# One fused kernel of attention with memory and a gated feed-forward: the hand-written order of GpSimd, VectorE and TensorE around the nested products is changed

## The chip, the cores and the metric

The kernel runs on one core of a Trainium2 chip. The metric is the device time of one execution, in microseconds (us); the number given for the kernel before is the median of three runs. One further execution was recorded by the hardware profiler, and all rows below come from it. The engines are named as the profile names them: PE is TensorE (PEld its weight loads), DVE is VectorE, ACT is ScalarE, POOL is GpSimd and SP is the engine that issues the transfers.

## The reference

The input x has 2048 rows of D = 576. Two branches are computed from it and mixed row by row by a gate:

```python
def _A_ref(x, wq, wk, wv, wo, beta):          # 32 heads of 18, 4 segments of 512 rows
    ...
    for s in range(N):
        qs, ks, vs = q[:, :, s], k[:, :, s], v[:, :, s]
        logits = jnp.einsum("bhqd,bhkd->bhqk", qs, ks) * scale + mask
        p = _softmax(logits, axis=-1)
        a_dot = jnp.einsum("bhqk,bhkd->bhqd", p, vs)
        pq = phi(qs)
        num = jnp.einsum("bhld,bhde->bhle", pq, M)
        den = jnp.einsum("bhld,bhd->bhl", pq, z)[..., None] + 1e-6
        a_mem = num / den
        o = g * a_mem + (1.0 - g) * a_dot
        outs.append(o)
        pk = phi(ks)
        M = M + jnp.einsum("bhld,bhle->bhde", pk, vs)
        z = z + jnp.einsum("bhld->bhd", pk)
    ...
    return o @ wo

def _B_ref(x, w_gate, w_up, w_down):          # F = 4608
    return (_gelu(x @ w_gate) * (x @ w_up)) @ w_down

g = _sigmoid((x * gate_w).sum(-1, keepdims=True))
return g * _A_ref(...) + (1 - g) * _B_ref(...)
```

The softmax is over the 512 keys of one segment; what lies before the segment enters through the memory M and its norm z.

## The kernel before, in words

All large products are made in 16-bit floats, and each 32-bit operand is split into two of them: a high half (a rounded copy, written by ACT) and a low half (the rest, written by POOL as operand minus high half). A pair of halves is what a product reads. "High" and "low" in a function's name (`high_g`, `low_g`, `high_d`, `low_d`, `hidden_pair`, `nest_pairs`) mean these two.

The program has three parts. At its start (to about 250 us) come the projections of the four segments, the memory and the pairs of x. The main part is a row of 72 steps, `step(v)`. Two steps make one block of 128 of the 4608 hidden columns (`f = v // 2`), over two row segments each (`p = v % 2`); four steps make a period (`fb = v // 4`, `i4 = v % 4`). Beside it each step from the fifth on works on one head of the attention, two tiles of it (`2k`, `2k + 1`, with `k = v - 4`). The last part holds what is left of the down product and the output projection.

In a step, PE makes the gate and up products of a block as seven products of a two-by-two split (A11, A12, A22, S1, S2, S4 and further sums of weights times x or sums of x; `product`, line 529) in the PSUM banks V, G (called X in the code) and U (called Y). DVE copies and adds them into the buffers `gl` (three of them) and `hold`, ACT takes the gelu in place, and `hidden` (DVE, line 1260) multiplies the up product in. `hidden_pair` (lines 1265 and 1266) then makes the two halves `hh` at the start of the next step, in `end_pair`.

For the blocks of even f the first product of a block is itself split once more (the nested variant): `nest(at, 0)` to `nest(at, 3)` are four pieces of it, made a step ahead in the steps i4 = 3 and i4 = 0, and `nest_last` is the fifth, made in the step that uses it. The pieces need sums of the raw weights (POOL, lines 327 to 387), and four nest pairs of these (`nest_pairs(b, i, "hl")`, high half on ACT in line 375, low half on POOL in line 377). The pieces gather in `hold0` (opened in step i4 = 3, read in the next period, and read last as a hidden tile in its fourth step) and `hold1`. There is one buffer of each. The first piece writes it with the copy in line 1361 of DVE.

The attention of a tile goes PE (scores, `st`/`dn` banks) -> DVE (maximum, line 1155) -> ACT (line 1166, `mb`; line 1171, the exponentials `pb`; line 1172, their high half `ph`) -> POOL (line 1173, low half) -> SP (transposing transfers) -> PE (values, line 1190). `powers(a)` is the part on ACT and POOL, `scores` and `put` that of PE and DVE, `values` the last.

The down product is cut into chains (`some(fb - 1, ...)`, 8 to a step, those of a period behind; line 1237), each of six matmuls and one eviction on DVE (line 1245). The down weights come by `load_d` (SP), are scaled by `scale_d` (DVE, line 391) and split by `high_d` and `low_d` (ACT line 395, POOL line 399); the buffers are two for the raw ones and four for the pairs. `squares` (ACT, line 89) gathers the column norms of coming weights and `scales` (PE, line 94, one matmul with ones) turns them into scale factors. `result_high` and `result_low` (ACT line 1214, DVE line 1220) split the attention's finished columns.

The order of work on PE, ACT, DVE and POOL is the order in which the code issues it: the program is built with a schedule written by hand for these four engines. Only SP's order is left to the scheduler. So a call that is moved in the code is moved on each of the four engines, and an engine never works past an instruction that waits.

## Time and profile before

| | us |
|---|---|
| median of three runs (lowest, highest) | 1604.89 (1604.72, 1605.11) |
| the profiled execution | 1603.99 |
| its span, first to last instruction | 1602.3 |
| PE busy | 1568.8 (98%) |
| PE weight loads busy | 953.8 (60%) |
| DVE busy | 1271.0 (79%) |
| ACT busy | 1208.5 (75%) |
| POOL busy | 1117.8 (70%) |

The granted TensorE clock is 0.999 on average. A row of a timeline gives start and duration in us, engine, line, operation, output and input, size and, in brackets, the idle time before it with what ended it; several like instructions in a row stand as one with a count. In the list of waits, the numbers are the total in us, how often, and the longest.

### The profile page before, as it was taken

The page shows a single profiled execution, that of the slowest core. Times are in us where ns is not written, and L with a number is a line of the kernel's source. Part 1 is how long each engine was busy: PE and PEld are TensorE (multiplying, and loading weights), DVE is VectorE, ACT ScalarE, POOL GpSimd, SP SyncE. Part 2 cuts the span into 40 slices and gives each one's busy share as a digit, 9 for nine tenths or more (in the row PEclk, how much of TensorE's full clock was granted, in tenths as well). Part 3 has the DMA queues.
Part 4 walks back from the last instruction along what each step waited for, and adds up shares of the span by engine and source line. Part 5 has one row for each costly group of instructions (what it writes and reads, how often), then busy time and mean ns, then how long its engine had stood idle before and what let it go on. Part 6 is the DMA issues. An engine that isn't in the chain of part 4 may idle for free. (4 is left out here: it accounts for less than half of the span.)

```text
span 1602.3 us, 33969 instructions
## 1 busy us (share of the span) xinstructions
PE 1568.8 (98%) x12220; PEld 953.8 (60%) x12220; DVE 1271.0 (79%) x3254; ACT 1208.5 (75%) x2059; POOL 1117.8 (70%) x1220
## 2 busy tenths in 40 slices
PE   9999998999999999999999999999999999999999
PEld 5665654565555555555565555555555556555577
DVE  6778975878788888888787878888888878787665
ACT  7567543879797889888887979788988888786421
POOL 5255555678686868686867868686868686776597
PEclk9999999999999999999999999999999999999999
DMA  6533332577776777777767778777777776764546
GB/s 228 208 123 130 124 122 56 112 117 133 130 135 127 131 142 131 126 138 125 134 128 131 129 129 138 130 136 134 138 130 140 127 138 131 131 115 92 119 85 168
DMA packets 472833, 209.97 MB, mean 131 GB/s; under 512 B 427688, under 2 KB 437416, under 8 KB 472152
## 3 DMA queue, kind: packets, MB, share of 16 engines
q1 hardware_dynamic: 472664, 207.80, 64.3%
q8 instruction: 96, 1.57, 0.4%
q14 instruction: 73, 0.60, 0.1%
HBM read 91.87 MB, written 27.26 MB: 74 GB/s over the span
## 5 line engine op out<-in xcount | busy, mean ns | idle before, releaser
L1173 POOL TENSOR_TENSOR pb<-pb,ph 128x896 f16<-128x896 f32 (+1 forms) x256 | 368.6, 1440 | 295.7 <-ACT ph L1172 285.6
L529 PEld LDWEIGHTS <-pairg 128*128 128x128 f16 x2592 | 249.3, 98 | 266.1 <-issue 27.6
L1237 PE MATMUL dn<-paird,hhr 128*128 128x288 f16 x2124 | 326.7, 286 | 0.3 <-DVE mx L1155 0.3
L1171 ACT ACTIVATE pb<-pb,mb,esc 128x512 f32<-128x512 f32 (+3 forms) x512 | 305.0, 642 | 5.3
L1245 DVE SCALAR_TENSOR_TENSOR acc<-dn,ev,acc 128x288 f32<-128x288 f32 x534 | 265.9, 513 | 42.3 <-PE dn L1237 34.4
L1237 PEld LDWEIGHTS <-hhr 128*128 128x128 f16 x2160 | 207.3, 98 | 87.8 <-issue 12.8
L529 PE MATMUL G<-x,pairg 128*128 128x512 f16 x864 | 211.1, 380 | 6.3 <-DVE gl L1260 6.3
L529 PE MATMUL U<-xt,pairg 128*128 128x512 f16 x864 | 209.9, 379 | 0.0
L1237 PE MATMUL dn<-paird,hhd 128*128 128x288 f16 x1272 | 204.8, 286 | 0.0
L1172 ACT ACTIVATE ph<-pb 128x896 f16<-128x896 f32 (+1 forms) x256 | 188.5, 736 | 8.1
L342 POOL TENSOR_TENSOR pairg<-raw,pairg 128x384 f16<-128x384 f32 (+2 forms) x144 | 158.5, 1122 | 13.9 <-ACT pairg L338 13.9
L1155 DVE CUSTOM_DVE_ANT_0 pb<-st,mask 128x512 f32<-128x512 f32 (+1 forms) x256 | 157.0, 613 | 0.0
L1237 PEld LDWEIGHTS <-hhd 128*128 128x128 f16 x1296 | 124.9, 98 | 49.8 <-issue 5.7
L1166 ACT ACTIVATE mb<-mx,esc 128x4 f32<-128x4 f32 x128 | 37.3, 291 | 149.2 <-DVE mx L1155 149.2
L1155 DVE CUSTOM_DVE_ANT_0 pb<-dn,mask 128x256 f32<-128x256 f32 (+1 forms) x192 | 67.1, 374 | 78.2 <-PE dn L1152 78.2
L1345 PE MATMUL V<-xt,nest 128*128 128x256 f16 x714 | 109.1, 273 | 13.1 <-POOL nest L377 12.2
L1269 ACT ACTIVATE gl<-gl,sc 128x512 f32<-128x512 f32 x110 | 75.2, 712 | 49.2 <-DVE gl L1513 37.6
L529 PE MATMUL V<-x,pairg 128*128 128x512 f16 x426 | 103.8, 379 | 2.4 <-DVE gl L1430 0.9
L529 PE MATMUL U<-x,pairg 128*128 128x512 f16 x432 | 105.0, 379 | 0.1
L1345 PEld LDWEIGHTS <-nest 128*128 128x128 f16 x714 | 64.4, 97 | 50.0 <-POOL nest L377 16.9
L1190 PEld LDWEIGHTS <-pt 128*128 128x128 f16 x2560 | 83.4, 96 | 5.5
L1266 POOL TENSOR_TENSOR hhr<-gl,hhr 128x512 f16<-128x512 f32 x67 | 78.6, 1183 | 11.5 <-ACT hhr L1265 11.5
(364 smaller groups left out, 3126.5 us busy)
## 6 DMA issues: line engine op xcount, KB each, us to landing
raw<-in_wgu_dram SPq DMA_DIRECT2D x36, 640.0 KB
rawd<-in_wd_dram SPq DMA_DIRECT2D x36, 288.0 KB
qt<-qk SPq DMA_DIRECT2D x132, 72.0 KB
kt<-qk SPq DMA_DIRECT2D x132, 72.0 KB
qk<-stage SPq DMA_DIRECT2D x36, 256.0 KB
qt<-qk SPq DMA_DIRECT2D x132, 36.0 KB
kt<-qk SPq DMA_DIRECT2D x132, 36.0 KB
vp<-vstage SPq DMA_DIRECT2D x16, 296.0 KB
```

The costliest lines, as they stand in the source:

```text
L342: pool.tensor_tensor(spot(f, *p, 1), raw_g[f][:, p[0] : p[1]], spot(f, *p, 0), OP.subtract)
L529: pe.matmul(o, w[:, i, (a + k) * P : (a + k + 1) * P], x[:, b + k], start=start and k == 0 and i == 0 and b == h, stop=k == 1 and i == 1, ...
L1155: dve.tensor_tensor_reduce(scored(a, qi), out[qi], mask[:, L - (qi + 1) * P :], 1.0, -3e38, OP.add, OP.max, mx[a][:, qi : qi + 1])
L1171: act.activation(r, r, AF.Exp, bias=b[:, qi : qi + 1], scale=esc[:, 0, c : c + 1])
L1172: act.activation(h[:, cols], p, AF.Copy)
L1173: pool.tensor_tensor(low[:, cols], p, h[:, cols], OP.subtract)
L1190: pe.matmul(ov, pr[:, 10 * i + COL[qi] // P + kb], v[:, 4 * e + kb, c0 : c0 + VC], start=kb == 0 and i == 0, stop=kb == qi and i == 1)
L1237: pe.matmul(o[:, :NH], hh[:, a, q * P : (q + 1) * P], w[:, b, n * NH : (n + 1) * NH], start=i == 0, stop=i == 5)
L1245: dve.scalar_tensor_tensor(av, o[:, :NH], ev, av, OP.mult, OP.add)
L1266: pool.tensor_tensor(hh[:, 1], t, hh[:, 0], OP.subtract)
L1269: act.activation(t, o, AF.Gelu_apprx_tanh, scale=scl[f // 2][0][:, 2 + c : 3 + c])
L1345: pe.matmul(o, w[:, (7 * c + i) * P : (7 * c + i + 1) * P], x[d], start=start and n == 0, stop=n == 2, skip_group_check=True)
```

## The change

It has six parts.

1. In the main part, the fourth step's start used to make the low halves of its two hidden tiles on POOL at once. Now `hidden_pair` may leave them (`wait=True`), and `hidden_lows` makes them after the step's `powers(2 * k - 1)`. The pair of down weights that was split in the third step is split in the fourth, with the other one. In the third step, the first two nest pairs and the sums that follow are made before `powers(2 * k)` instead of after; the third pair comes at the end of the third step, the fourth in the fourth step behind the hidden lows.
2. The down weights are loaded in the first step of their own period, both, instead of in the third and fourth step of the period before.
3. `result_low` is issued one step sooner, in the third step instead of the fourth.
4. In the steps i4 = 0 and 1, two chains follow the last nested piece, instead of one there and one further on.
5. `scales` of the next period is called after the next product and chain instead of before.
6. In the first period the nest pairs are made at the end of step 2 and the hidden low of step 2 behind them; the nest pieces of step 3 come one place later each; the first down weights are split at step 3's start; among the first projections, two value weights are split by other engines and one query/key pair is split in two calls.

The diff, with comments and the parts that only rename left out:

```diff
@@ make_v, the first projections
-            if k < 3:
+            if k not in (2, 3):
                 pair_of(t, r, sc)
                 return
...
-                    if 2 <= j < 6:
+                    if j == 4:
+                        make_qk(7, pair_high)
+                        finish_later()
+                        make_qk(7, pair_low)
+                    elif 2 <= j < 6:
                         make_qk(j + 3)
...
-                    if 1 <= j < 6:
+                    if 1 <= j < 5:
                         make_v(j - 1)
+                    if j == 4:
+                        make_v(4)
@@ hidden_pair
-        def hidden_pair(f, c, t):
+        def hidden_pair(f, c, t, wait=False):
             slot = hh_slot[f, c] = hh_free.pop(0)
             hh = hp[f, c] = hh_tile(slot)
             act.activation(hh[:, 0], t, AF.Copy)
-            pool.tensor_tensor(hh[:, 1], t, hh[:, 0], OP.subtract)
+            lows.append((hh, t))
+            if not wait:
+                hidden_lows()
+
+        def hidden_lows():
+            while lows:
+                hh, t = lows.pop(0)
+                pool.tensor_tensor(hh[:, 1], t, hh[:, 0], OP.subtract)
@@ weights_nest
-            if i4 == 2 and at == 2:
+            if i4 == 2 and at == "late":
                 for i in range(2):
                     nest_pairs(fb + 1, i, "hl")
                 nest_sums(fb + 1)
+            if i4 == 2 and at == 2:
+                for i in (2,) if fb else (2, 3):
+                    nest_pairs(fb + 1, i, "hl")
             if i4 == 3 and at == 0:
-                for i in (2, 3):
-                    nest_pairs(fb + 1, i, "hl")
+                hidden_lows()
+                if fb:
+                    nest_pairs(fb + 1, 3, "hl")
@@ weights_low, weights_load
-            if i4 >= 2:
-                low_d(n0 + i4 - 2)
+            if i4 == 3:
+                for f in (n0, n0 + 1):
+                    low_d(f)
...
-            if i4 == 2:
-                load_d(n0 + 2)
+            if i4 == 0 and fb:
+                load_d(n0)
+                load_d(n0 + 1)
             if i4 == 3:
                 load_g(n0 + 5)
-                load_d(n0 + 3)
@@ step
-            low = (k - 7) // 4 if k % 4 == 3 and 0 <= (k - 7) // 4 < H // 2 - 1 else None
+            low = (k - 6) // 4 if k % 4 == 2 and 0 <= (k - 6) // 4 < H // 2 - 1 else None
...
-            end_pair()
+            end_pair(i4 == 3 and fb > 0)
             if v == 3:
                 high_g(2, 1)
                 low_g(2, 1)
+                for n in range(2):
+                    high_d(n)
+                    low_d(n)
...
-            if v != 4:
-                some(fb - 1, early[:1])
+            one = 2 if fb and i4 < 2 else 1
+            some(fb - 1, early[:one])
...
-            if v in (2, 3):
-                nest_pairs_x(v - 2, 1)
+            if v == 2:
+                nest_pairs_x(0, 1)
             weights_nest(fb, i4, 1)
-            if v == 3:
-                nest(at, 0)
-            some(fb - 1, early[0 if v == 4 else 1 : 2])
+            some(fb - 1, early[one:2])
...
-            if v == 0 or fb > 1 and i4 == 1:
+            if v == 0:
                 scales(fb + 1)
                 scales_out(fb + 1)
...
             if v == 3:
-                nest(at, 1)
+                nest(at, 0)
             some(fb - 1, early[2:3])
-            if v == 5:
-                scales(2)
-                scales_out(2)
+            if fb and i4 == 1:
+                scales(fb + 1)
+                scales_out(fb + 1)
             product(Y, f, S1, t, 0, 2)
             rest(Y, f, G4, x2_, (0,) if fb else (0, 1))
+            if v == 3:
+                nest(at, 1)
...
-            if v == 3:
-                nest(at, 2)
             if not fb:
                 hidden(f, c, X, g0)
-                hidden_pair(f, c, g0)
+                hidden_pair(f, c, g0, v == 2)
...
             product(Y, f, S4, x2_, 2, 6)
+            if v == 3:
+                nest(at, 2)
...
             put(2 * k, 2)
             puts.pop(2 * k, None)
+            weights_nest(fb, i4, "late")
             if on(k):
                 powers(2 * k)
...
             ends.append((f, e, Y, g1))
+            if v == 3:
+                nest_pairs_x(1, 1)
             weights_nest(fb, i4, 2)
+            if v == 2:
+                hidden_lows()
```

How this moves instructions is seen at three places of a period from the middle of the main part. The first is POOL at the end of the third step and in the fourth (`pb` are the attention's low halves, `hhr` the hidden ones, `nest` the nest pairs' low halves; numbers tell buffers' uses apart). Before:

```order
L387 TENSOR_TENSOR raw<-raw 128x128
L1266 TENSOR_TENSOR hhr_11682<-gl,hhr_11682 128x512
L1266 TENSOR_TENSOR hhr_11685<-hold_10728,hhr_11685 128x512
L1173 TENSOR_TENSOR pb_11648<-pb_11648,ph 128x896
L1173 TENSOR_TENSOR pb_11648<-pb_11649,ph 128x384
L377 TENSOR_TENSOR nest<-nest 128x256
L377 TENSOR_TENSOR nest<-raw,nest 128x256
L342 TENSOR_TENSOR pairg<-raw,pairg 128x384
```

And now:

```order
L387 TENSOR_TENSOR raw<-raw 128x128
L1179 TENSOR_TENSOR pb_11542<-pb_11542,ph 128x896
L1179 TENSOR_TENSOR pb_11542<-pb_11543,ph 128x384
L377 TENSOR_TENSOR nest<-nest 128x256
L1179 TENSOR_TENSOR pb_11656<-pb_11656,ph 128x896
L1179 TENSOR_TENSOR pb_11656<-pb_11657,ph 128x384
L1281 TENSOR_TENSOR hhr_11684<-gl,hhr_11684 128x512
L1281 TENSOR_TENSOR hhr_11686<-hold_10727,hhr_11686 128x512
L377 TENSOR_TENSOR nest<-raw,nest 128x256
```

The hidden tiles' low halves went from ahead of the tile's attention product to behind it, the other tile's attention product from before the nest's first pairs (not shown) to behind them, and the two later nest pairs apart from each other.

The second is ACT in the third step, up to the attention's `mb` (waits in brackets). Before:

```order
L395 ACTIVATE paird<-rawd 128x576
L1269 ACT_TABLE_LOAD
L1269 ACTIVATE hold_10728<-hold_10728,sc 128x512 [waits DVE_49]
L1269 ACTIVATE gl<-gl,sc 128x512 [waits DVE_49]
L1166 ACTIVATE mb<-mx,esc 128x4 [waits DVE_49]
L1171 ACT_TABLE_LOAD [waits DMAHW3_49,Activation_49]
```

And now:

```order
L395 ACTIVATE paird<-rawd 128x576
L1284 ACT_TABLE_LOAD
L1284 ACTIVATE hold_10727<-hold_10727,sc 128x512 [waits DVE_49]
L1284 ACTIVATE gl<-gl,sc 128x512 [waits DVE_49]
L375 ACTIVATE nest<-raw 128x256 [waits Pool_49]
L375 ACTIVATE nest<-nest 128x128 [waits Pool_49]
L1172 ACTIVATE mb<-mx,esc 128x4 [waits DVE_49]
```

The high halves of the first two nest pairs, which wait for POOL, now stand ahead of `mb`.

The third is DVE in the fourth step, from the attention's maximum to the first hidden product of the pair. Before:

```order
L1361 COPY hold_11852<-V 128x256 [waits PE_49,Pool_49]
L1245 SCALAR_TENSOR_TENSOR acc<-dn,ev,acc 128x288 [waits PE_49]
L1155 ISA pb_11811,mx<-st,mask 128x384
L1155 ISA mx 128x1
L1364 COPY hold_11852<-V 128x256 [waits PE_49]
L1365 COPY V<-V 128x256 [waits DVE_49]
L1245 SCALAR_TENSOR_TENSOR acc<-dn,ev,acc 128x288 [waits PE_49] x2
L1369 TENSOR_TENSOR hold_11852<-V,hold_11852 128x256 [waits PE_49]
L1220 SCALAR_TENSOR_TENSOR ob<-ob,wsc,oh 128x576
L1260 SCALAR_TENSOR_TENSOR gl<-G,sc,gl 128x512 [waits PE_49,Activation_49]
```

And now:

```order
L1381 COPY hold_11851<-V 128x256 [waits PE_49,Activation_49,Pool_49]
L1251 SCALAR_TENSOR_TENSOR acc<-dn,ev,acc 128x288 [waits PE_49]
L1161 ISA pb_11810,mx<-st,mask 128x384
L1161 ISA mx 128x1
L1384 COPY hold_11851<-V 128x256 [waits PE_49]
L1385 COPY V<-V 128x256 [waits DVE_49]
L1251 SCALAR_TENSOR_TENSOR acc<-dn,ev,acc 128x288 [waits PE_49] x2
L1389 TENSOR_TENSOR hold_11851<-V,hold_11851 128x256 [waits PE_49]
L1266 SCALAR_TENSOR_TENSOR gl<-G,sc,gl 128x512 [waits PE_49,Activation_49]
```

The result's low half (L1220) left its place ahead of the hidden product. The copy into the hold buffer waits for POOL before and now; the last POOL reader of that buffer is the second of the two hidden low halves above (`hold_10728` before, `hold_10727` now, the same single buffer).

More of the change, by code (lines that the diff above doesn't have):

```diff
@@ L1260, in hidden @@
             dve.scalar_tensor_tensor(t, o, sc[:, 6 + c : 7 + c], t, OP.mult, OP.mult)
-        def hidden_pair(f, c, t):
+        lows = []
+        def hidden_pair(f, c, t, wait=False):
             slot = hh_slot[f, c] = hh_free.pop(0)
@@ L1381, in end_first, with end_pair @@
             ends[0] = ends[0] + (True,)
-        def end_pair():
+        def end_pair(wait=False):
             for i, g in enumerate(ends):
@@ L1392, in end_pair @@
             for f, c, o, g, *_ in ends:
-                hidden_pair(f, c, g)
+                hidden_pair(f, c, g, wait)
             ends.clear()
@@ L1514, in step @@
             gelu(f, e, g1, g1)
-            if v == 3:
-                for n in range(2):
-                    high_d(n)
-                    low_d(n)
             if fb:
@@ L1526, in step @@
                 normalize(k - 2)
-            if v == 3:
-                nest(at, 2)
             if not fb:
                 hidden(f, c, X, g0)
-                hidden_pair(f, c, g0)
+                hidden_pair(f, c, g0, v == 2)
                 if v < 3:
```

## The prediction

> **What bounds the kernel now.** I read the page's busy shares first, then the waits of PE, then one period of four steps in the timeline. One matrix engine does nearly everything:
>
> ```profile
> span 1602.3 us, 33969 instructions
> PE 1568.8 (98%) x12220; PEld 953.8 (60%) x12220; DVE 1271.0 (79%) x3254; ACT 1208.5 (75%) x2059; POOL 1117.8 (70%) x1220
> ```
>
> PE is idle for 33.5 us of the span, so that is about all that a change of order can win. The waits of PE say where:
>
> ```profile
> PE V L1345 <- POOL nest L377: 12.2, 17, 4.9
> PE G L529 <- DVE gl L1260: 6.3, 17, 0.4
> PE dn L94 <- ACT nest L89: 3.2, 15, 0.2
> ...
> PE dn L419 <- POOL wv L606: 0.8, 1, 0.8
> ```
>
> Sixteen of the first wait, fifteen of the second and third come once in each period of four steps; the longest, 4.9 us, is step 3. One period, from its third step's end to the next period's start, on PE:
>
> ```profile
> 854.90 0.71 PE L1345 MATMUL V<-xt,nest 128*128 128x256 f16 x5
> 856.09 0.28 PE L1345 MATMUL V<-xt,nest 128*128 128x256 f16 x1 [0.48 <-POOL nest L377]
> 856.96 0.49 PE L1345 MATMUL V<-xt,nest 128*128 128x256 f16 x3
> 860.94 0.66 PE L1190 MATMUL pv<-vt,pt 128*128 128x37 f16 x20
> 861.97 1.46 PE L529 MATMUL G<-x,pairg 128*128 128x512 f16 x6 [0.38 <-DVE gl L1260]
> 863.59 0.90 PE L1237 MATMUL dn<-paird,hhr 128*128 128x288 f16 x6
> 864.54 1.46 PE L529 MATMUL V<-x,pairg 128*128 128x512 f16 x6
> ```
>
> The idle time in brackets leaves out the drain of the matmuls before it, so I count starts. Three nest matmuls start over 0.33 us, twenty pv over 0.50, six dn over 0.73. The nest's sixth matmul then comes 0.64 late, G 0.53 late, and V after the chain 0.22 late.
>
> **The change, part by part.** Three losses are removed by moving work.
>
> First, G waits for DVE, which stands on the result's low half before the hidden product:
>
> ```profile
> 860.45 0.81 DVE L1220 SCALAR_TENSOR_TENSOR ob<-ob,wsc,oh 128x576 f16<-128x576 f32 x1
> 861.18 0.74 DVE L1260 SCALAR_TENSOR_TENSOR gl<-G,sc,gl 128x512 f32<-128x512 f32 x1
> 863.79 0.69 DVE L1430 COPY gl<-V 128x512 f32<-128x512 f32 x1 [0.33 <-PE V L1345]
> ...
> 841.27 0.75 DVE L1260 SCALAR_TENSOR_TENSOR gl<-G,sc,gl 128x512 f32<-128x512 f32 x1 [0.37 <-PE G L1279]
> 842.68 1.46 PE L529 MATMUL G<-x,pairg 128*128 128x512 f16 x6
> ```
>
> The 0.81 goes to the step before, ahead of that step's hidden product, which DVE starts at 841.27 after 0.37 idle. So it starts 0.44 later and ends at 842.46, and PE writes G again at 842.68: covered by 0.2 us, I cost it at nothing, and at 0.4 per period if that cover is gone. Gain 15 x 0.54 = 8.1 us.
>
> Second, V waits for the copy L1430, which ends 0.69 after 863.79, at 864.48. With two chains (1.47 us) instead of one, PE arrives at 865.06. The second chain is taken from ahead of the next product, where six matmuls (1.46 us with the last one's end) still cover DVE's 0.69 copy. Gain 0.21 x 32 steps = 6.7 us.
>
> Third, the scales' sum (L94) waits for ACT's squares:
>
> ```profile
> 812.21 0.90 PE L1237 MATMUL dn<-paird,hhd 128*128 128x288 f16 x6
> 813.32 0.39 PE L94 MATMUL dn<-stat,ones 128*128 128x10 f32 x2 [0.21 <-ACT nest L89]
> ```
>
> It is 813.32 - 812.94 = 0.38 late and moves behind eight matmuls and a chain, about 2.25 us. Gain 15 x 0.38 = 5.7 us.
>
> The fourth edit is GpSimd's order, and it is the one in question. It removes the nest's stall of 0.64 x 16 = 10.2 us, since the third pair's low half is there long before. But it also puts the low half of the hidden tile that lies in the hold buffer behind both attention products. That buffer is single, and the copy at line 1361 (1381 now), which opens the next hold, waits for GpSimd. So I follow GpSimd and ACT through it:
>
> ```profile
> 838.84 1.28 POOL L399 TENSOR_TENSOR paird<-rawd,paird 128x576 f16<-128x576 f32 x1
> 840.08 0.74 POOL L327 TENSOR_TENSOR raw<-raw 128x256 f32<-128x256 f32 x1
> 844.29 2.89 POOL L1173 TENSOR_TENSOR pb<-pb,ph 128x896 f16<-128x896 f32 x2
> 850.29 1.16 POOL L1266 TENSOR_TENSOR hhr<-gl,hhr 128x512 f16<-128x512 f32 x1
> 851.40 1.16 POOL L1266 TENSOR_TENSOR hhr<-hold,hhr 128x512 f16<-128x512 f32 x1
> 855.36 0.67 POOL L377 TENSOR_TENSOR nest<-nest 128x256 f16<-128x256 f32 x1
> ...
> 839.91 0.30 ACT L1166 ACTIVATE mb<-mx,esc 128x4 f32<-128x4 f32 x1 [0.53 <-DVE mx L1155]
> 843.01 0.95 ACT L1172 ACTIVATE ph<-pb 128x896 f16<-128x896 f32 x1
> 845.30 0.40 ACT L375 ACTIVATE nest<-raw 128x256 f16<-128x256 f32 x1
> 845.60 0.29 ACT L375 ACTIVATE nest<-nest 128x128 f16<-128x128 f32 x1
> 845.80 0.61 ACT L1265 ACTIVATE hhr<-gl 128x512 f16<-128x512 f32 x1
> 846.84 0.28 ACT L1166 ACTIVATE mb<-mx,esc 128x4 f32<-128x4 f32 x1
> 848.60 0.95 ACT L1172 ACTIVATE ph<-pb 128x896 f16<-128x896 f32 x1
> ...
> 856.48 0.42 DVE L1361 COPY hold<-V 128x256 f32<-128x256 f32 x1 [1.05 <-PE V L1345]
> ```
>
> - GpSimd's sums move up by the removed L399, 1.24 us: they took 840.08 to 844.29, and now end at 843.05.
> - ACT's first two nest halves now stand ahead of the attention's mb, and the second waits for those sums. So mb starts near 843.34, not 839.91: **3.43 us later**.
> - From mb to the end of the first ph is 4.05 us: 847.39. GpSimd's attention product takes 847.46 to 850.30 (2.84 of its 2.89 us pass before the next one starts). The third pair's low half follows and is done at 850.94, not 856.03.
> - ACT's attention block takes 5.39 us (839.91 to 845.30), then one nest half (0.31) and two hidden halves (1.04): the second mb is at 850.08, its ph ends 2.71 later, at 852.79.
> - GpSimd's second product: 852.87 to 855.71. Only now come the two hidden low halves, 2.23 us: **857.94**. Before they ended at 852.5.
> - The copy, for which PE is ready at 855.84 (856.48 less 0.64) when the nest's stall is gone, starts at 858.00 and PE's next nest matmuls 0.48 after it, as the rows of before have it: 858.5. Before it was 856.96, so this place gets 1.57 us longer although the old stall is gone. PE's new wait is 858.5 - 856.3 = **2.2 us**.
>
> Queued behind the copy on DVE stand a chain's eviction, half of an attention maximum and two more copies, 2.3 us in all; PE waits for the first copy alone, since twelve dn matmuls and twenty pv (1.47 + 0.50 us) stand between its second and its third nest piece, and the piece itself takes 0.33. Price: 16 x 1.57 = +25.1 us. From below: if ACT's and GpSimd's blocks pack tighter by 1.57 us, nothing; from above, if DVE's work stretches GpSimd's two products by a tenth each, 0.6 us: 9.3 us more.
>
> **Step 3**, where the first hold is opened, is separate. The last two rows are stretches of time: length, then busy us (and instructions) of PE, its weight loads, DVE, ACT and GpSimd, the granted clock, the DMA share and GB/s:
>
> ```profile
> 251.80 0.39 PE L1345 MATMUL V<-xt,nest 128*128 128x256 f16 x2 [0.60 <-ACT nest L375]
> 257.12 0.40 PE L1345 MATMUL V<-xt,nest 128*128 128x256 f16 x1 [4.93 <-POOL nest L377]
> 257.31 2.77 PE L529 MATMUL G<-x,pairg 128*128 128x512 f16 x6
> 268.06 1.46 PE L529 MATMUL V<-x,pairg 128*128 128x512 f16 x6 [0.85 <-DVE gl L1430]
> 253.17:256.58 3.41, 0.00 (x0) 0.00 (x0) 1.39 (x1) 0.25 (x1) 3.41 (x4) 1.00 0.00 0
> 256.58:260.00 3.42, 2.88 (x8) 1.17 (x9) 0.42 (x1) 0.00 (x0) 1.15 (x2) 0.50 0.30 64
> ```
>
> The waits cost 0.60 + 4.93 + 0.85, and 1.31 (2.77 less 1.46) for six matmuls at the granted clock 0.50: 7.7 us. Now the pairs are made in step 2, but a deferred hidden low half (1.16 us in the rows above) stands behind them on GpSimd, and the step's first U copy on DVE waits for it. From above all 7.7 us are won; from below nothing, if the waits only move. I take two waits in their place, each of one low half and one DVE copy (1.16 + 0.69 = 1.85 us): at the product that writes U again, and at the next one, which the nest's own copies stand ahead of. They are the nearest rows, and both too short for the clock to fall as it did. Gain 7.7 - 3.7 = 4.0 us.
>
> The down weights' loads go from the third and fourth step to the first one of their own period. ACT's squares read them in the second step, about a quarter period after the issue; I cost them at nothing, and if they land late it is the squares, and ACT's attention block behind them, that wait. The reorder among the first projections concerns the 0.8 us that PE waits for value weights from GpSimd. PE's next work there hangs on DVE's staging, which is not shortened: I cost it at nothing, at best 0.8.
>
> Sum: +25.1 - 8.1 - 6.7 - 5.7 - 4.0 = **+0.6 us**. The profiled execution took 1603.99 (span 1602.3); the median of the runs is 1604.89, 0.9 above. Forecast: no change, **1605.5 us**.
>
> The stretch at clock 0.50 began after a window of 3.41 us without one matmul. The Trainium skill (TensorE: Matmul & The Clock Gate, What's actually happening) says that the clock halves after at least one whole idle window of some 3.4 us; the trace agrees at step 3. By that rule a wait of 2.2 us cannot halve it, and the sum stands; it speaks against the second rival below.
>
> **The rivals.** *The new wait is short or hidden*: ACT and GpSimd finish the attention products some 2 us sooner than in my chain. For it: mb in before sat 0.53 us idle and the chain assumes that nothing else gives. Against it: every link is a start-to-start distance of the trace. Then the period loses 0.64 + 0.54 + 0.42 + 0.38 = 1.98 us, 16 x 1.98 + 4.0 = 36: **1569 us**; with half the wait, **1587**.
>
> *The clock falls (slower)*: if PE's 2.2 us wait, once in each period, draws a half-clock window as 4.93 us did, each costs up to 1.31 us more: 16 x 1.31 = +21, **1626 us**. It decides only when the wait covers a window; against it, the waits are 1.2 us short of one.
>
> *The small waits come back*: V, G and L94 wait for the same amount at the next place, since DVE and ACT have the same work. Then 20.5 us of gain shrinks to half: **1615 us**. Against it: DVE shows idle time of 1.05 and 0.33 us right there.
>
> **How the numbers follow.** What a measurement can tell from no change is about 0.2%, 3.2 us. The new wait has an error of 0.3 us in sixteen periods, 4.8 us. The forecast's case has 0.65: of it 0.33 within 0.2%, 0.18 faster, 0.14 slower. The short wait has 0.17, all faster; the clock 0.08, slower; the returning waits 0.10, slower but for 0.02. In all: faster 0.35, same 0.35, slower 0.30. The likeliest case alone spans 1597 to 1613; the range, with the half wait and the returning waits, 1586 to 1616.
>
> **What would show it.** Right: PE waits of about 2.2 us sixteen times at the nest, put down to the hold copy, the copy waiting for GpSimd's hidden low half; mb of the first head some 3.4 us later; no G, V and L94 waits; step 3's wait below 4 us and no half clock. Wrong: nest waits under 1 us (then faster), or a granted clock of 0.50 inside the periods (then slower).

## The result and the profile after

The changed kernel takes **1623.03 us** (median; 1622.6 to 1623.15), the kernel before 1604.83 in the same runs. The ratio is 1.0113, 95% interval 1.0095 to 1.013: 18.2 us slower, where no change was forecast (1605.5 us, with 1586 to 1616 as the range). The profiled execution's span grew from 1602.3 to 1621.3 us, by 19.0.

The page's head and the list of PE's waits (total us, times, longest) of the changed kernel:

```profile
span 1621.3 us, 33956 instructions
PE 1564.1 (96%) x12220; PEld 957.2 (59%) x12220; DVE 1275.8 (79%) x3254; ACT 1211.2 (75%) x2059; POOL 1124.0 (69%) x1220
...
PE V L1365 <- DVE hold L1381: 37.7, 16, 2.5
PE dn L1243 <- DVE mx L1161: 5.9, 16, 1.0
PE U L529 <- DVE gl L1536: 1.6, 1, 1.6
PE U L529 <- DVE gl L1501: 1.3, 1, 1.3
```

The old list is gone: no nest pair, no L94, no copy before V, and of the hidden product only 0.6 us. In its place stands the hold copy, sixteen times, as the prediction had it, and a wait that it did not have: a down chain that waits for the attention's maximum, also once in a period.

What releases the hold copy is seen in the timelines of one period (start, duration, engine; idle time before it in brackets), ordered here by engine (ACT, POOL, DVE, PE). PE's wait is 2.44 to 2.48 us, as here, at thirteen of the sixteen places, and 1.73 to 2.07 us at the other three:

```profile
467.64 0.31 ACT L375 ACTIVATE nest<-nest 128x128 f16<-128x128 f32 x1 [2.69 <-POOL nest L365]
467.86 0.28 ACT L1172 ACTIVATE mb<-mx,esc 128x4 f32<-128x4 f32 x1
474.53 0.28 ACT L1172 ACTIVATE mb<-mx,esc 128x4 f32<-128x4 f32 x1
...
465.38 1.12 POOL L331 TENSOR_TENSOR raw<-raw 128x256 f32<-128x256 f32 x1
477.32 2.89 POOL L1179 TENSOR_TENSOR pb<-pb,ph 128x896 f16<-128x896 f32 x2 [1.89 <-ACT ph L1178]
481.27 1.16 POOL L1281 TENSOR_TENSOR hhd<-hold,hhd 128x512 f16<-128x512 f32 x1
...
464.84 1.08 DVE L1226 SCALAR_TENSOR_TENSOR ob<-ob,wsc,oh 128x576 f16<-128x576 f32 x1
482.46 0.42 DVE L1381 COPY hold<-V 128x256 f32<-128x256 f32 x1 [3.02 <-POOL hhd L1281]
...
482.94 0.49 PE L1365 MATMUL V<-xt,nest 128*128 128x256 f16 x3 [2.47 <-DVE hold L1381]
```

It is the chain of the prediction, link by link: ACT's second nest half waits 2.69 us for GpSimd's sums and mb stands behind it; GpSimd's second attention product waits for its ph; the hold's hidden low half is last; the copy waits for it, PE for the copy. At this place it is 0.4 us longer than reckoned, and the row of L331 says where: one of the sums took 1.12 us, not 0.73, and it began while DVE made the result's low half that the change had moved there (L1226, itself 1.08 us instead of 0.81).

The wait on the maximum comes from a small operation of the scales (the last row is the same line in the kernel before):

```profile
440.37 1.81 DVE L270 TENSOR_SCALAR pb<-z 128x4 int32<-128x4 int32 x1
442.29 0.42 DVE L1161 CUSTOM_DVE_ANT_0 pb<-dn,mask 128x256 f32<-128x256 f32 x1
...
440.25 2.90 POOL L1179 TENSOR_TENSOR pb<-pb,ph 128x896 f16<-128x896 f32 x2 [0.22 <-ACT ph L1178]
...
442.77 0.90 PE L1243 MATMUL dn<-paird,hhr 128*128 128x288 f16 x6 [0.29 <-DVE mx L1161]
...
814.62 0.17 DVE L270 TENSOR_SCALAR pb<-z 128x4 int32<-128x4 int32 x1
```

Four numbers a partition take DVE 1.81 us; the same line took 0.17 us in the kernel before. It starts 0.12 us after GpSimd's attention product. The maximum behind it on DVE is late, and the chain that writes the same PSUM bank again waits.

Periods differ, too. Rows of stretches (length, then busy us and instructions of PE, weight loads, DVE, ACT and GpSimd, the granted clock, DMA share, GB/s); the first two are whole periods, the others neighbouring windows of 3.41 us:

```profile
404.88:480.47 75.59, 72.83 (x605) 44.04 (x604) 61.61 (x164) 63.57 (x108) 55.80 (x60) 1.00 0.73 131
632.71:709.88 77.17, 74.43 (x604) 44.86 (x604) 61.29 (x164) 63.68 (x108) 55.77 (x60) 0.98 0.70 125
478.34:481.75 3.41, 2.13 (x16) 1.40 (x15) 1.10 (x4) 3.39 (x6) 3.33 (x4) 1.00 0.94 93
481.75:485.16 3.41, 2.22 (x32) 1.88 (x32) 2.66 (x8) 2.65 (x5) 3.41 (x5) 1.00 0.70 157
631.94:635.35 3.41, 0.96 (x9) 0.66 (x7) 0.67 (x2) 3.38 (x5) 3.41 (x5) 1.00 1.15 130
635.35:638.76 3.41, 3.41 (x23) 2.27 (x22) 1.97 (x7) 2.65 (x5) 3.41 (x4) 0.50 0.60 127
```

A plain period is 75.59 us (74.58 before). Four of the sixteen waits are followed by 3.413 us at clock 0.50, and such a period is about 1.5 us longer: 6 us in all. The four stretches start at multiples of 3.4133 us from each other (45, 134 and 201 of them from the first). So the windows run on by themselves, and a wait of this length counts when it falls into one of them (the window from 631.94), not when a border cuts it (the wait from 480.47, cut at 481.75).

### The profile page after: what moved, and what is told of

It reads as the page before. It is cut to its first block, busy times and chain, and to the rows that moved or that the text cites. A ratio compares the mean times of both kernels' runs of the same rounds, so it can differ in the third digit from the quotient of the medians.

```text
span 1621.3 us, 33956 instructions
## 1 busy us (share of the span) xinstructions
PE 1564.1 (96%) x12220; PEld 957.2 (59%) x12220; DVE 1275.8 (79%) x3254; ACT 1211.2 (75%) x2059; POOL 1124.0 (69%) x1220
## 3 DMA queue, kind: packets, MB, share of 16 engines
q8 instruction: 96, 1.57, 0.4%
## 4 chain that ended last, share of the span: by engine, by line
PE 71%; DVE 9%; POOL 8%; ACT 5%; issue 3%; DMA 3%; SPq 0%; DVEq 0%; POOLq 0%; ACTq 0%
PE dn L1243 19%; PE U L529 12%; PE G L529 8%; PE V L529 5%; PE V L1365 4%; PE pv L1196 4%; POOL pb L1179 3%; PE st L409 2%; PE dn L416 2%; DVE pb L270 1%; PE U L1289 1%; PE G L1294 1%; PE G L409 1%; PE U L409 1%; ACT ph L1178 1%
## 5 line engine op out<-in xcount | busy, mean ns | idle before, releaser
L1251 DVE SCALAR_TENSOR_TENSOR acc<-dn,ev,acc 128x288 f32<-128x288 f32 x534 | 263.7, 513 | 39.1 <-PE dn L1243 33.1
L1365 PE MATMUL V<-xt,nest 128*128 128x256 f16 x714 | 107.1, 275 | 38.0 <-DVE hold L1381 37.7
```

The source lines that it names most:

```text
L1251: dve.scalar_tensor_tensor(av, o[:, :NH], ev, av, OP.mult, OP.add)
L1365: pe.matmul(o, w[:, (7 * c + i) * P : (7 * c + i + 1) * P], x[d], start=start and n == 0, stop=n == 2, skip_group_check=True)
```

## The experiments

Each was timed beside the kernel before on the same chip (1604.9 to 1605.3 us there). Where an expectation speaks of "the run before this one", it means the run that it names in brackets behind these words.

### What makes the hold copy wait

**The low halves at once.** In the changed kernel the deferral of the hidden low halves in the fourth step is taken back:

```diff
-            end_pair(i4 == 3 and fb > 0)
+            end_pair()
```

> The changed kernel, but the fourth step's hidden low halves are made at the step's start again, not behind both attention products; everything else stays changed. My theory (the hold copy waits for the deferred low half): the sixteen waits of 2.47 us go, and with them the four half-clock windows; 1623 - 16 x 2.64 - 6 = about 1575 us, no wait at the hold copy above 0.3 us, the waits on the attention maximum (5.9 us) remain. Rival (the nest pairs ahead of the attention in the third step are what makes the copy late, since they hold mb back by 3.9 us): the wait stays above 2 us and the time above 1610 us.

Measured: 1594.57 us, ratio 0.9934 (0.992 to 0.9949). The hold waits and all half-clock stretches but one are gone, and yet 20 us of the expected gain are missing. The list of waits and one place of PE's timeline:

```profile
PE pv L1196 <- DMA pt<-pb: 13.5, 13, 2.0
...
408.60 0.64 PE L1196 MATMUL pv<-vt,pt 128*128 128x37 f16 x19 [0.89 <-DMA pt<-pb]
```

Both theories were half right. The copy waits for the deferred low half, but the attention really is late, and with the first wait gone PE's value products wait for the transposing transfers. The long wait had hidden that.

**The hold's low half first.** The order of the two deferred halves is turned round:

```diff
             for f, c, o, g, *_ in ends:
                 hidden_pair(f, c, g, wait)
+            if wait:
+                lows.reverse()
             ends.clear()
```

> The changed kernel with the two deferred low halves in the other order: the hold tile's first, the other one after it. My theory: the hold copy is released one low half (1.11 us) sooner, PE's wait is 1.36 us instead of 2.47, none of the sixteen waits is followed by a half-clock window (none fills more than 1.9 us of one window), time 1623 - 16 x 1.11 - 6 = about 1599 us. Rival (attention lateness): the wait and the time stay as they are, 1623 us. If half-clock windows came from something other than the idle time, they would remain, four or so, and the time would be 1605 us.

Measured: 1607.09 us, ratio 1.0016 (1.0006 to 1.0025), 8 us above the expectation. The wait does what the theory says, and no half-clock stretch is left inside the periods; the rest is again value products that wait for transfers (5.7 us), and waits on the maximum as in the changed kernel (6.0 us):

```profile
PE V L1365 <- DVE hold L1381: 20.3, 16, 1.4
PE pv L1196 <- DMA pt<-pb: 5.7, 8, 1.1
```

**The first pairs back.** Only the "late" call goes behind the first tile's `powers` again:

```diff
-            weights_nest(fb, i4, "late")
             if on(k):
                 powers(2 * k)
+            weights_nest(fb, i4, "late")
```

> The changed kernel with the first two nest pairs and the sums behind the first tile's attention product again (third step), the low halves still deferred. Theory now: the second tile's mb is late because the third pair's high half stands ahead of it on ACT and waits for GpSimd's sums; with the pairs back these sums end only some 3 us after the first product (about 0.3 us sooner than in the changed kernel), so the hold copy still waits 2.0 to 2.5 us and the time is 1615 to 1625 us. Rival: it is the first tile's mb, 3.9 us late, that makes all late; with it on time the wait is below 0.6 us and the time about 1585 us.

Measured: 1619.89 us, ratio 1.0092 (1.0075 to 1.0109); the wait is 2.36 us on average. The theory holds. ACT and the waits of this run:

```profile
473.05 0.42 ACT L375 ACTIVATE nest<-nest 128x256 f16<-128x256 f32 x1 [3.14 <-POOL nest L385]
474.41 0.28 ACT L1172 ACTIVATE mb<-mx,esc 128x4 f32<-128x4 f32 x1
...
PE V L1365 <- DVE hold L1381: 37.8, 16, 2.4
```

With the first mb on time, the second is late all the same: ahead of it on ACT stands the third nest pair's high half, which the change moved from behind the second attention to before it, and which waits 3.14 us for GpSimd.

**Attention first.** On top of the run with the pairs back, the third pair goes behind the second attention as well, and the hold's low half comes first of the two:

```diff
-                for i in (2,) if fb else (2, 3):
+                for i in () if fb else (2, 3):
                     nest_pairs(fb + 1, i, "hl")
             if i4 == 3 and at == 0:
+                if fb:
+                    nest_pairs(fb + 1, 2, "hl")
+                lows.reverse()
                 hidden_lows()
```

> As the run with the pairs back, and the third nest pair behind the second tile's attention (as before the change), then the hidden low halves, the hold's first, then the fourth pair. Theory: both tiles' mb stand at the times of the kernel before, GpSimd's second product starts when its ph is there and not behind the hidden lows, the third pair is 2.5 us sooner than before, the hold's low half ends about 1 us ahead of the copy: no wait at the hold copy or at the nest above 0.2 us, no values waiting for transposes, no half-clock window. 1623 - 42 - 6 = 1575 us, the waits on the attention maximum still there (about 8 us in all). Rival (the deferral itself cannot be covered): a hold wait of 1 us or more remains, 1590 us or more.

Measured: **1576.65 us**, ratio 0.9819 (0.9805 to 0.9834): 28.7 us faster than the kernel before and 46.4 faster than the changed one, within 2 us of the expectation. GpSimd, DVE and the largest wait that is left:

```profile
469.30 2.88 POOL L1179 TENSOR_TENSOR pb<-pb,ph 128x896 f16<-128x896 f32 x2
472.77 1.16 POOL L1281 TENSOR_TENSOR hhd<-hold,hhd 128x512 f16<-128x512 f32 x1
...
475.12 0.42 DVE L1384 COPY hold<-V 128x256 f32<-128x256 f32 x1 [0.42 <-POOL hhd L1281]
...
PE dn L1243 <- DVE mx L1161: 5.8, 17, 1.0
```

The second attention product no longer waits for its ph (no idle time before it at 469.30), the hold's low half ends at 473.93, and the nest does not appear in the list of waits. The row of the copy puts its idle time down to GpSimd, but the hold's half was done 1.19 us before; the copy starts 0.14 us after the end of the matmuls whose result it takes (474.98). The gain over the changed kernel is what was found there: 40.4 us of the hold wait with its drain, and 6.0 of half clock. So the deferral can be had without a wait; it was the nest pairs' high halves ahead of both mb that made it dear. The turned order of the two low halves is hardly needed for it: by the same rows the hold's half would otherwise end 1.1 us later, at 475.05, still ahead of the copy. The deferral alone, in the kernel before, was not run.

### The clock

**One low half more** ahead of the hold's, to make the wait longer:

```diff
-            while lows:
+            for again in range(len(lows)):
                 hh, t = lows.pop(0)
-                pool.tensor_tensor(hh[:, 1], t, hh[:, 0], OP.subtract)
+                for _ in range(2 if lows and not again else 1):
+                    pool.tensor_tensor(hh[:, 1], t, hh[:, 0], OP.subtract)
```

> The changed kernel with the first of the two deferred low halves written twice on GpSimd (1.11 us more ahead of the hold's low half). PE's wait becomes 2.47 + 1.11 = 3.58 us, 17.8 us more in sixteen periods. What the clock does then tells two readings apart. Mostly idle is enough (in the changed kernel a window of the 3.413 us lattice with 2.37 us idle or more was followed by a half-clock window, one with 1.89 or less was not): about 11 to 13 of the sixteen waits leave a window that idle, each costs 1.5 us, so 8 more half windows and 1623 + 18 + 12 = about 1653 us. Only a window without any matmul counts: none or one of sixteen, and the time is 1635 to 1641 us.

Measured: 1661.35 us, ratio 1.0348 (1.0331 to 1.0366). All sixteen waits (3.7 us) are followed by a half-clock stretch, more than either reading had. The run hardly tells the two apart, since in fourteen of the sixteen windows PE is idle for 3.36 us or more of the 3.41:

```profile
486.46:489.87 3.41, 0.00 (x0) 0.00 (x0) 0.44 (x2) 2.40 (x3) 3.33 (x4) 1.00 0.66 138
489.87:493.28 3.41, 3.37 (x15) 2.21 (x15) 2.25 (x6) 2.41 (x4) 3.41 (x5) 0.50 0.28 57
```

The stretches start exactly 23 windows apart (78.51 us): period and windows have locked to each other, which no reading had foreseen. What tells the readings apart are the other runs. Over the changed kernel and the runs with the pairs back and with the scales back, a window with 2.13 us or more of one wait in it (thirteen of them, up to 2.47) was always followed by clock 0.50, and one with 1.97 us or less never. The two nearest to the border are both in the run with the pairs back; idle is 3.41 less PE's busy time:

```profile
631.87:635.28 3.41, 1.28 (x11) 1.07 (x11) 1.73 (x6) 2.69 (x5) 3.41 (x5) 1.00 0.66 138
635.28:638.70 3.42, 3.42 (x34) 2.09 (x33) 1.58 (x4) 3.38 (x4) 3.29 (x3) 0.50 0.45 156
935.66:939.07 3.41, 1.45 (x13) 1.18 (x13) 1.89 (x6) 2.69 (x5) 3.41 (x5) 1.00 0.97 157
939.07:942.48 3.41, 3.41 (x62) 2.48 (x60) 2.77 (x7) 3.37 (x5) 3.15 (x3) 1.00 0.49 183
```

In the run with the low halves at once, one window with a wait of 1.91 us was followed by it too:

```profile
554.43:557.84 3.41, 1.50 (x29) 1.00 (x26) 2.30 (x8) 3.37 (x5) 1.86 (x3) 1.00 1.03 228
557.84:561.25 3.41, 3.41 (x13) 1.77 (x12) 0.83 (x2) 2.21 (x5) 3.33 (x3) 0.50 1.72 277
```

Twenty of its 29 matmuls are the small value products of 37 columns each, so idle time alone is not what decides. A count that does fit is the columns that PE's matmuls write in a window (512 for a 128x512 output; a matmul on a border is shared out by time). In the fourteen traces, behind the first 60 us and up to the last 4, every window with about 2,800 columns or fewer was followed by clock 0.50, and none with about 3,200 or more; none lies between. The window above has some 2,600. The count is an estimate: another way of sharing out the matmuls on a border blurs the limit by some 200 columns. No run was made to test it.

### The scales' small operations

**The scales back** at their old place in the changed kernel:

```diff
-            if v == 0:
+            if v == 0 or fb and i4 == 1:
                 scales(fb + 1)
                 scales_out(fb + 1)
...
-            if fb and i4 == 1:
-                scales(fb + 1)
-                scales_out(fb + 1)
             product(Y, f, S1, t, 0, 2)
```

> The changed kernel with the scales' sum and what follows it (six small DVE operations, six small GpSimd ones) back ahead of the third product of the second step; nothing else. My theory: the waits of PE on the attention maximum (16 times, 5.9 us and 2.7 us of drain) come from one small DVE operation that takes 1.81 us instead of 0.17 while GpSimd's attention product runs; at the old place they fall into GpSimd's short sums, and those waits go; PE's wait at L94 does not come back in full, since the squares are done 0.1 us ahead by the two chains moved. 1623 - 8.6 + at most 4 = 1615 to 1619 us. Rival (the maxima are late for another reason, the scores being issued earlier than DVE can follow): the waits stay, and L94 waits 0.38 again: 1623 to 1629 us.

Measured: 1628.46 us, ratio 1.0144 (1.0129 to 1.0159), 5.4 us slower than the changed kernel. The waits on the maximum are gone, as the theory says, but L94 waits again, and more than before:

```profile
PE dn L94 <- ACT nest L89: 7.0, 16, 0.8
```

The expectation had the squares done 0.1 us ahead, and that was wrong: as much of PE's work stands ahead of L94 as in the kernel before, less V's 0.21 us, so PE comes that much sooner and waits 0.4 us for squares that end where they ended. Six half-clock stretches instead of four add 3 us, which no theory had in it. So with the two chains moved ahead of it, the scales' move gains some 2 us (5.4 less 3); the next run shows it alone.

**The scales alone**, moved in the kernel before:

```diff
-            if v == 0 or fb > 1 and i4 == 1:
+            if v == 0:
                 scales(fb + 1)
                 scales_out(fb + 1)
...
-            if v == 5:
-                scales(2)
-                scales_out(2)
+            if fb and i4 == 1:
+                scales(fb + 1)
+                scales_out(fb + 1)
             product(Y, f, S1, t, 0, 2)
```

> The kernel before with one edit alone: the scales' sum a product and a chain later in the second step. By the prediction's third term, 1605 - 5.7 = 1599 us. By what the runs so far show of the small DVE operations (one of them 1.8 us long once GpSimd's attention product runs), the L94 wait is exchanged for a wait on the attention maximum of the same size: 1603 to 1608 us.

Measured: 1614.08 us, ratio 1.0056 (1.0041 to 1.0071): 9 us slower, worse than either had it. Its waits, and DVE and GpSimd at one place:

```profile
PE dn L1237 <- DVE mx L1155: 14.3, 16, 0.9
...
820.50 1.89 DVE L266 TENSOR_SCALAR z<-x,z 128x4 f32<-128x4 f32 x1
822.50 0.89 DVE L271 TENSOR_SCALAR v<-v 128x2 int32<-128x2 int32 x1
...
820.48 2.88 POOL L1173 TENSOR_TENSOR pb<-pb,ph 128x896 f16<-128x896 f32 x2 [0.23 <-ACT ph L1172]
```

Here two operations are held, the first until about the end of GpSimd's first instruction (of 896 columns), the second until that of its second. So the price depends on which of the six operations meets the product, and the third term of the prediction is a loss by itself.

**The scales still later**, behind the step's down chains, on the attention-first kernel:

```diff
-            if fb and i4 == 1:
-                scales(fb + 1)
-                scales_out(fb + 1)
             product(Y, f, S1, t, 0, 2)
...
             some(fb - 1, early[3:])
+            if fb and i4 == 1:
+                scales(fb + 1)
+                scales_out(fb + 1)
             put(2 * k, 3)
```

> The run before this one (attention first) and the scales' sum with its small operations still later in the second step, behind its down chains, where GpSimd has no attention product running. Theory: the small DVE operations take 0.15 to 0.25 us each, the waits on the maximum (5 to 6 us and 2.7 us of drain) are gone: 8 us less than the run before this one, about 1567 us. Rival (these operations stretch wherever they stand): the waits move to another consumer, and the time stays within 2 us of that run.

Measured: 1587.19 us, ratio 0.9887 (0.9873 to 0.9902): 10.5 us slower than attention first. The waits on the maximum are gone, and the small operations take 0.15 to 0.60 us, but L94 writes a bank of the down chains, and behind three chains it waits for their evictions:

```profile
PE dn L94 <- DVE acc L1251: 12.6, 15, 0.9
```

**Step 2's low half at once**, on top of that (`hidden_pair(f, c, g0)` in place of `hidden_pair(f, c, g0, v == 2)`):

> The run before this one (scales later), and step 2's hidden low half at once instead of behind the nest pairs. Theory: step 3's first U copy on DVE does not wait for it (1.3 us of PE's wait and part of the 1.6 us of the next one go), the nest pairs come 1.2 us later, which step 3 covers: 1 to 3 us less. Rival: the nest's pieces wait instead, no change or 1 us more.

Measured: 1585.44 us, ratio 0.9877 (0.9862 to 0.9892), 1.75 us less than the run before it, within what was expected: the wait of 1.3 us at the U copy is gone. The one of 1.6 us, of which a part was to go, stays.

**The scales one chain sooner**, on the attention-first kernel with step 2's low half at once:

```diff
+            if fb and i4 == 1:
+                scales(fb + 1)
+                scales_out(fb + 1)
             some(fb - 1, early[2:3])
-            if fb and i4 == 1:
-                scales(fb + 1)
-                scales_out(fb + 1)
```

> Attention first (1576.7 us), with step 2's hidden low half at once and the scales' sum ahead of the third chain of the second step instead of behind it, so that its six small DVE operations come 0.4 us sooner, between GpSimd's last short sum and its attention product. Theory: all are done before that product holds them, the sixteen waits on the maximum (5.8 us and 2.7 us of drain) go, 1576.7 - 8 - 1.5 = 1567 us. Rival: one of them still falls into the product and takes 1.8 us, 1575 us.

Measured: 1576.19 us, ratio 0.9828 (0.9812 to 0.9845): the rival. At the place shown five operations in a row are done in time, and the last is held as another was elsewhere. The eviction (L1251) behind it on DVE is late, and the waits on the maximum are exchanged for eight longer ones on it:

```profile
434.77 1.87 DVE L272 TENSOR_SCALAR pb<-pb 128x4 int32<-128x4 int32 x1
...
PE dn L1243 <- DVE acc L1251: 8.3, 8, 1.5
```

### The other terms alone

**The result's low half sooner**, in the kernel before:

```diff
-            low = (k - 7) // 4 if k % 4 == 3 and 0 <= (k - 7) // 4 < H // 2 - 1 else None
+            low = (k - 6) // 4 if k % 4 == 2 and 0 <= (k - 6) // 4 < H // 2 - 1 else None
```

> The kernel before with one edit alone: the result's low half one step sooner on DVE. The prediction's first term by itself: the wait of G on the hidden product (6.3 us with its drain 8.1) goes, 1605 - 8 = 1597 us; rival: the 0.81 us delays the hidden product of the third step and its consumer waits instead, 1603 us or more.

Measured: 1605.69 us, ratio 1.0003 (0.9993 to 1.0012): nothing. The wait of G is gone, but the nest's wait has grown from 12.2 to 19.7 us. The waits, GpSimd and DVE of this run:

```profile
PE V L1345 <- POOL nest L377: 19.7, 16, 4.9
...
842.52 1.34 POOL L329 TENSOR_TENSOR raw<-raw 128x256 f32<-128x256 f32 x1
...
842.47 0.81 DVE L1220 SCALAR_TENSOR_TENSOR ob<-ob,wsc,oh 128x576 f16<-128x576 f32 x1
```

GpSimd's sum beside it takes 1.34 us, not 0.73. The 0.6 us go down GpSimd's chain to the nest pair, and PE's wait for that pair is 7.5 us longer in all. The move costs no wait on DVE, as the prediction had it, but it costs GpSimd.

**Two chains behind the nested piece**, in the kernel before:

```diff
-            if v != 4:
-                some(fb - 1, early[:1])
+            one = 2 if fb and i4 < 2 else 1
+            some(fb - 1, early[:one])
...
-            some(fb - 1, early[0 if v == 4 else 1 : 2])
+            some(fb - 1, early[one:2])
```

> The kernel before with one edit alone: two chains behind the last nested piece in the first two steps, none between the next two products. The prediction's second term by itself: V's 0.21 us behind the copy goes in 32 steps, 1605 - 6.7 = 1598 us, unless the L94 wait, which the moved chain used to shorten by 0.73 us once a period, grows by that (16 x 0.73 would eat it: 1605 us or more). Rival to the term: the 0.21 us is drain that is there whatever stands before V, no change.

Measured: 1600.04 us, ratio 0.9969 (0.9957 to 0.998): 4.9 us faster. V no longer waits. PE comes sooner to L94 for it, and that wait grows to about 0.4 us each, by 2.6 us in all, which covers the 1.8 us that are missing to the term:

```profile
PE dn L94 <- ACT nest L89: 5.8, 14, 0.4
```

## Why the prediction was wrong

The wait that decides was found, with its place and its count. The time was missed because three prices were: of the 18.4 us between the sum (+0.6) and the measured +19.0 of the span, 5.1 are the hold wait, 7.1 the scales and 6.0 the clock.

- **The hold wait** (term +25.1 us): right in kind, too small. PE's start came 2.6 us late at thirteen places (2.44 to 2.48 us idle, 0.17 of drain), against 2.2. Sixteen waits of 37.7 us and 2.7 of drain, less the 10.2 of the old wait, make +30.2. The step that failed is that GpSimd's sums were carried over at their old duration, while the change puts DVE's 0.81 us beside them; the prediction allowed for DVE stretching the attention products, and only as a bound. The term has a small slip too: by its own rows the place gets 858.48 - 856.96 = 1.52 us longer, not 1.57, so that it should have been +24.3.
- **The scales, L94** (-5.7): wrong in sign. The step that failed is that the six small DVE operations behind the sum were moved past GpSimd's short sums to its attention product and costed at nothing. The old wait went, with some 1.5 us more for the second of L94's two matmuls, which the term had left out (the pair took 0.39 us at 813.32 and 0.28 at 439.23); 5.9 us on the maximum with 2.7 of drain came: +1.4. In its outcome this is the third rival for one term; the rival's reason, the same work at the next place, is not what the rows show, since one operation takes ten times as long there.
- **The clock**, priced as a rival at 21 us with a chance of 0.08: it fell in four of sixteen periods, 1.5 us each, +6.0 us. The step that failed is "a wait of 2.2 us cannot halve it", which was drawn from the rule cited there and from a window without any matmul, the only case that the trace showed.
- **G behind the result's low half** (-8.1): the wait went as reckoned. That it would be "covered" was argued from DVE's queue alone; alone in the kernel before, the edit gains nothing, since it comes back through GpSimd. In the changed kernel that is the excess of the hold wait above.
- **V behind the copy** (-6.7): the wait went; alone the edit brought 4.9 us.
- **Step 3** (-4.0): right in kind, and 1 us more. The G product of step 4 starts at 261.35 and not at 265.42, 4.1 us sooner, with waits of 1.26 and 1.57 us where two of 1.85 were assumed, and no half clock; the wait of V behind it (0.85 us) is gone as well, and the next G product is 5.0 us sooner (267.29 and 272.33).

Sum: 30.2 - 8.1 - 6.7 + 1.4 + 6.0 - 5.0 = +17.8 us against 19.0 measured in the span; 1.2 us are not placed. Among them are two short waits that the kernel before did not have, 0.5 us on an eviction and 0.3 on a transfer. The down weights' loads and the first projections, both costed at nothing, were not run alone.

The rival in which the wait is short did not come true, but its size was about right: freed of the wait by order alone, the kernel takes 1576.65 us, between its two prices of 1569 and 1587.

## What to carry to other kernels

An operation that is moved takes its cost along to whatever runs beside it there: before a move between DVE and GpSimd, look at what the other of the two does in that stretch, and price the longest of its instructions. When short work is put ahead of a latency chain, follow what it waits for; here copies of 0.3 to 0.4 us held both attention chains, since they waited for another engine. And when a long wait goes, the next list of waits has to be worked out anew, since it hides what is late behind it.

## What the runs showed of the hardware that was not expected

**DVE and GpSimd hold each other.** Small DVE operations of 0.15 to 0.23 us took 1.81, 1.87 and 1.89 us when they met GpSimd's instruction of 896 columns, and ended within 0.03 us of it; GpSimd's sum of 0.73 us took 1.12 and 1.34 us beside a DVE operation with two inputs in SBUF. The price is up to the rest of the other engine's instruction. Not every DVE operation is held: those that read or write a PSUM bank beside the same product in the changed kernel (471.93 to 473.81) took no longer than elsewhere, such as

```profile
472.60 0.21 DVE L1207 RECIPROCAL ord<-pv 128x8 f32<-128x8 f32 x1
```

The Trainium skill (GPSIMD Engine Reference, Specifications) says that the two engines share their SBUF interfaces and that DVE instructions in a two-port mode or with two SBUF inputs contend for them. The stretched sums beside the result's low half, which has two such inputs, agree; whether the held small operations, with one input tensor each, run in a two-port mode, no trace here shows.

**The clock halves after a window that is only mostly idle.** The windows are 3.4133 us long and free-running; among the long waits at the hold copy, 2.13 us in one window was enough, 1.97 was not, and a count of the columns written fits all traces. The Trainium skill (TensorE: Matmul & The Clock Gate, What's actually happening) has the window's length and that it runs free, which the traces confirm, but speaks of an idle window; here the measurement decides. With waits of 3.7 us the kernel's period locked to 23 windows (78.51 us).
